# Attention halves in two pieces, value sums queued earlier, and new task rates in a fused attention and two-MLP kernel

## The chip, the core and the metric

The kernel runs as one program on one core of a Trainium2 chip. The metric is the device time of one execution in microseconds. Before the change the median of three runs is 1530.74 us (1528.70, 1530.74 and 1532.65).

## The reference

```
# q, k, v: 8 batches x 8 heads x 576 tokens x 64
k_p, v_p = means of k and v over groups of 8 tokens      # 72 rows each
attn = softmax(q @ k_p^T / 8)                            # 576 x 72 for each head
x = attn @ v_p, heads side by side                       # 4608 tokens x 512
x2 = ((x @ w1) * (x @ w2)) @ w3 @ w_out                  # 512 -> 1024 -> 1024 -> 512
out = square(relu(x2 @ w_in)) @ w_out2                   # 512 -> 2048 -> 512
```

All inputs and the output are float32.

## The kernel before

Tokens are worked on in 9 blocks of 512 (TB). Most products are made of three matmuls of a split operand: a value is a rounded part and a rest, each in the format F32R, and high x high, high x rest and rest x high are added up (mm3). Before anything else, w3 and w_out are folded into one matrix (fold). Then each block goes through the first MLP: stage_ab makes the two products with w1 and w2 (ps_w, 8 units of 48 matmuls), and stage_w multiplies with the folded matrix (acc, 12 matmuls a unit, two units later). After the ninth block comes the second MLP, with the lines L1117 and L1219; no attention work is left then.

Attention fills x between the blocks' matmuls. A batch has 576 tokens and a block has 512, so their borders don't agree. A batch is cut into two halves of 256 and 320 tokens, five query tiles in all. For a query tile there are two score tasks (pe_s: 4 matmuls ps_s each, maxima on DVE at L482, exponentials on ACT at L485) and two transposing tasks (pe_t: ps_t at L521 and L526). For a half there are four AV tasks (pe_av), one for each pair of heads: three matmuls with the split of v (vl, L193) and one with rows of v that don't fit in 128 partitions (vr, L541). Their result is copied by ACT (L554) and subtracted by DVE (L557) into x, which is done apart for each block that the half touches. ps_s, ps_t and ps_av share two PSUM buffers (ps_at).

All order is made while the program is written out. The matmuls of the blocks call tick() after each six. A tick adds `rate` to a credit (attend, L658); from a credit of `visit` on (2.0 while the blocks run), tasks are taken from the front of one list while the credit lasts, one credit each. A task has conditions in a set of things issued, and a task at the front whose condition is not met holds all that stand behind it. An AV task's conditions are ("v", b), that v of its batch has been cut into vl and vr, and ("ab", n), that block n has been issued: x has buffers for two blocks, so the tokens of block m wait for block m - 2. The condition is taken from the half's last token:

```
need = [("v", b)]
last = (b * S + s_end(hf) - 1) // TB
if last >= 2:
    need.append(("ab", last - 2))
```

A block begins when all AV tasks that touch its tokens have been issued (tokens_ready, L674); until then bare ticks are made, which bring tasks alone. The compiler may move instructions of one engine past each other where their data allow it.

v is prepared by kv_parts and load_v (L357): one part at a tick, from a queue that k shares, loads a tile of v (SP's queue) or sums one over groups of 8 (DVE, L329; the odd rows at L325). cut (L366) and cut_odd (L370) then split the sums into vl and vr on ACT (L362, L375) and DVE (L363). load_v(b + 1) is called behind the last AV of batch b (L645). The buffers of raw tiles (three) are shared with the loads of the second MLP's weights, which are converted on ACT and DVE beside the blocks and stored by SP.

The rate is 0.5 at the end of the folding, 0.7 from the point at which block 0 can begin, and 0.6 from the end of block 1 on.

Of the kernel before, what the change touches and what calls it, by code (L numbers as in the profile page):

```python
# [16 lines left out]
TB = 512  # L17
# [18 lines left out]
def attn_moe_moe2_kernel(  # L36
# [17 lines left out]
    B, H, S, D = q.shape  # L54
# [6 lines left out]
    NP = H // 2  # L61
# [8 lines left out]
    QT = []  # L70
    s0 = 0
# [3 lines left out]
    HALF = [[0, 1], [2, 3, 4]]  # L75
    HWS = [sum(QT[i][1] for i in h) for h in HALF]
# [23 lines left out]
    done = set()  # L100
# [85 lines left out]
    def mm3(ps, pairs, first=True, last=True):  # L186

        todo = []
        for (ah, al), (bh, bl) in pairs:
            todo += [(ah, bh), (ah, bl), (al, bh)]  # L190
        n = len(todo)
        return [
            (lambda a=a, b=b, i=i: nc.tensor.matmul(  # L193
                ps, a, b, start=first and i == 0, stop=last and i == n - 1))
            for i, (a, b) in enumerate(todo)
        ]
# [48 lines left out]
    vp = at_p.tile([P, NP, D], F32, tag="vp", name="vp")  # L245
# [4 lines left out]
    vr = at_p.tile([RR, NP, 2, D], F32R, tag="vr", name="vr")  # L250
# [106 lines left out]
    def load_v(b):  # L357


        def parted(hi, lo, src, row):  # L360

            nc.scalar.activation(hi, src, ACTF.Copy, scale=row)  # L362
            nc.vector.scalar_tensor_tensor(  # L363
                lo, src, row, f32(hi), op0=ALU.mult, op1=ALU.subtract)

        def cut():  # L366
            for x in range(2):
                parted(vl[:, 0, :, x, :], vl[:, 1, :, x, :], vp, rows[:, x:x + 1])

        def cut_odd():  # L370
            vo = vr.rearrange("p (a b) t d -> p b a t d", a=2)[:, :, :, 1]
            for x in range(2):
                row = rows[:RB, 2 + x:3 + x]
                parted(vo[:RB, x], vo[2 * RB:, x], v5, row)
                nc.scalar.activation(vo[RB:2 * RB, x], v5, ACTF.Copy, scale=row)  # L375
            done.add(("v", b))

        return kv_parts(v, b, lambda j: vp[:, j, :], [cut, cut_odd])

    def pe_kt(b, part):  # L380

# [148 lines left out]
        if 2 * len(QT) <= g < NG - 1:  # L530
            place_rem(g + 1)

    def pe_av(b, hf, hp):
        hi, lo, rem = atts[b, hf]
        s0 = QT[HALF[hf][0]][0]
        w = sum(QT[i][1] for i in HALF[hf])
        ps = ps_at.tile([P, TB], F32, tag="at", name="ps_av")
        st = [vl[:, i, hp].rearrange("p a d -> p (a d)") for i in range(2)]
        for m in mm3(ps[:, :w], [(st, [t[:, hp, :w] for t in (hi, lo)])], last=False):
            m()  # L540
        nc.tensor.matmul(  # L541
            ps[:, :w], vr[:, hp].rearrange("p a d -> p (a d)"), rem[:, hp // 2, :w],
            start=False, stop=True)
        t0 = b * S + s0
        pieces = []
        o = 0
        while o < w:
            blk, c = divmod(t0 + o, TB)
            n = min(w - o, TB - c)
            pieces.append((blk, c, o, n))  # L550
            o += n

        for blk, c, o, n in pieces:
            nc.scalar.copy(xt_tile(blk, hp)[:, 0, c:c + n], ps[:, o:o + n])  # L554
        for blk, c, o, n in pieces:
            t = xt_tile(blk, hp)
            nc.vector.tensor_sub(t[:, 1, c:c + n], ps[:, o:o + n], f32(t[:, 0, c:c + n]))  # L557
        done.add(("av", b, hf, hp))

    NG = B * len(QT)  # L560

    def s_end(hf):
        return QT[HALF[hf][-1]][0] + QT[HALF[hf][-1]][1]

    def build_tasks(first_k, first_v):


        order = []
        pend = []

        def put(fn, need=()):
            order.append((need, fn))

        def put_pend(n=1):
            for _ in range(min(n, len(pend))):
                order.append(pend.pop(0))

        def kt(b):
            for part in range(2):
                put(lambda part=part: pe_kt(b, part), [("k", b)])  # L580

        def sc(g):
            for half in range(2):
                put(lambda half=half: pe_s(g, half))
                put_pend()

        def turns(g):
            b, i = divmod(g, len(QT))
            for hf, tiles in enumerate(HALF):
                if b < EARLY and i == tiles[0]:  # L590
                    for x in tiles:
                        put(lambda hf=hf, x=x: turn_q(b, hf, x))

        def ahead_of(g):
            b, i = divmod(g, len(QT))
            at = (len(QT) if b + 1 < EARLY else HALF[1][0], len(QT))
            early = b + 1 < EARLY
            if i + 1 == at[0] and b + 1 < B:
                put(lambda b=b: load_q(b + 1, 0))
            if i + 1 == at[1] and b + 1 < B:  # L600
                if not early:
                    put(lambda b=b: load_q(b + 1, 1))
                kt(b + 1)
            if g + 1 < NG:
                turns(g + 1)
                sc(g + 1)
            if i + 1 == at[1] and early:
                put(lambda b=b: load_q(b + 1, 1))

        for fn in first_k:  # L610
            put(fn)
        kt(0)
        turns(0)
        sc(0)
        for g in range(NG):
            b, i = divmod(g, len(QT))
            hf = 0 if i in HALF[0] else 1

            if g < 2 * len(QT):
                if g + 1 != len(QT):  # L620
                    ahead_of(g)
            else:
                if g == 2 * len(QT):
                    ahead_of(g)
                if g + 1 < NG:
                    ahead_of(g + 1)
            if i == HALF[hf][0]:
                put_pend(len(pend))
            for part in range(2):
                put(lambda g=g, part=part: pe_t(g, part))  # L630
                put_pend()
            if g == 0:
                for fn in first_v:
                    put(fn)
            if i == HALF[hf][-1]:
                need = [("v", b)]

                last = (b * S + s_end(hf) - 1) // TB
                if last >= 2:
                    need.append(("ab", last - 2))  # L640
                for hp in range(NP):
                    def av(b=b, hf=hf, hp=hp):
                        pe_av(b, hf, hp)
                        if hf == 1 and hp == NP - 1 and b + 1 < B:
                            load_v(b + 1)  # L645
                    pend.append((need, av))
                if b < EARLY:
                    put_pend(len(pend))
            if g + 1 == len(QT):
                ahead_of(g)  # L650
        put_pend(len(pend))
        return order

    credit = [0.0]
    rate = [0.0]
# [17 lines left out]

    def tokens_ready(n):  # L674

        b, s = divmod(n, S)
        halves = [(bb, h) for bb in range(b) for h in range(2)]
        if s:
            halves.append((b, 0))
            if s > QT[HALF[1][0]][0]:  # L680
                halves.append((b, 1))
        return all(("av", bb, h, hp) in done for bb, h in halves for hp in range(NP))


    wt = {}
# [311 lines left out]
    last = NB - 1  # L997
# [334 lines left out]
    hold_v[0] = False  # L1332
    pumps.append(feed_w12)
    until(lambda: tokens_ready(TB))
    rate[0] = 0.7
    visit[0] = 2.0

    late = []
# [26 lines left out]
    for step in order:  # L1365
# [4 lines left out]
        elif step[0] == "ph":  # L1370
            names, x = plain_units(step[2])
            useq.extend([(n, x) for n in names])
    pend = []
    for i in range(NB):
        until(lambda: tokens_ready((i + 1) * TB))
        keep_q[0] = i > 0
        for u in range(U1):
            stage_ab(i, u)
            if i == last and u == TB // P - 1:
                for n in ("B11", "T1", "T2", "T3"):  # L1380
                    for x in range(2):
                        x2o[n, x] = w0_p.tile([P, 2, TB], F32R, tag="w", name="x2o")
                raw_x.append(x_p.tile([P, 2, TB], F32, tag="x", name="x2r"))
                for n in ("B21", "B22", "T4"):
                    for x in range(2):
                        x2o[n, x] = x_p.tile([P, 2, TB], F32R, tag="x", name="x2o")
                more = x_p.tile([P, 2, TB], F32, tag="x", name="gx")
                operands.extend(operands_of(0))
                tail = operands[-2:]
                del operands[-2:]  # L1390
            if len(pend) == LAG:
                stage_w(*pend.pop(0))
            pend.append((i, u))
        done.add(("ab", i))
        if i == 1:
            rate[0] = 0.6
        if i == 0:
            until(lambda: not fh1)
            sec_p.release()
            ring.append(tc.alloc_tile_pool(name="ring", bufs=RING, reuse_waits="tile"))  # L1400
# [104 lines left out]
```

## Time and profile before

| what | us |
|---|---|
| median of three runs | 1530.74 |
| the profiled execution, time | 1529.85 |
| its span | 1528.0 |
| TensorE (PE) busy | 1492.2 |
| VectorE (DVE) busy | 1000.3 |
| ScalarE (ACT) busy | 798.4 |
| GpSimd (POOL) busy | 81.2 |

Times in the trace count from the span's start. A row of the timeline gives the start, the duration of a group of like instructions, the engine, the line, the operation, what it writes and reads, the shape and the number; in brackets stands how long the engine was idle before it and what it waited for. PEld is TensorE's loading of weights, which lies beside its matmuls. PEclk is the granted share of TensorE's clock.

### The profile page before, as it was taken

The numbers are of one execution on the slowest core, as the hardware profiler recorded it, in microseconds if no ns is written. First come the engines' busy times: TensorE is split into PE (matmuls) and PEld (weight loads), VectorE is DVE, ScalarE is ACT, GpSimd is POOL, SyncE is SP. The second block draws the span as 40 slices with busy tenths as digits, with TensorE's granted clock in tenths as the row PEclk, the third lists the DMA queues.
The fourth block names the chain that finished last, engine by engine and source line by source line (L and its number), as shares of the span: only waits on it lengthen the run. The fifth ranks groups of instructions, "written<-read, shape, count | busy, mean of one in ns | idle before, by whom it ended". The sixth has DMA issues, their size and how long they took to land.

```text
span 1528.0 us, 21290 instructions
## 1 busy us (share of the span) xinstructions
PE 1492.2 (98%) x6752; PEld 1200.6 (79%) x6752; DVE 1000.3 (65%) x1798; ACT 798.4 (52%) x1953; POOL 81.2 (5%) x144
## 2 busy tenths in 40 slices
PE   6899999999999999999999999999999999999998
PEld 3457778877888888878888888888888888888887
DVE  7988686676767477658245477759675967576542
ACT  6866465454545355545235575456445744464431
POOL 1011110101010011100000000000000000000000
PEclk9999999999999999999999999999999999999999
DMA  9545666566666657557539777777777777788752
GB/s 288 197 139 138 165 196 161 168 178 174 187 199 174 193 127 242 149 169 227 173 113 307 222 195 247 208 209 229 235 207 208 232 207 207 208 268 282 209 163 89
DMA packets 292783, 301.34 MB, mean 197 GB/s; under 512 B 119360, under 2 KB 184896, under 8 KB 292672
## 3 DMA queue, kind: packets, MB, share of 16 engines
q1 hardware_dynamic: 287488, 290.54, 65.3%
q10 hardware_dynamic: 5184, 9.44, 1.8%
q8 instruction: 55, 0.90, 0.2%
q14 instruction: 56, 0.46, 0.1%
HBM read 243.27 MB, written 56.62 MB: 196 GB/s over the span
## 4 chain that ended last, share of the span: by engine, by line
PE 71%; DVE 4%; ACT 2%; DMA 1%; issue 1%; ACTq 0%; DVEq 0%
PE o L1219 18%; PE ps_w L193 17%; PE acc L193 9%; PE ps_c L1117 5%; PE ps_a L1117 5%; PE ps_d L1117 5%; PE ps_h L193 3%; PE o L193 3%; PE ps_b L1117 3%; PE ps_s L468 1%; PE ps_av L193 1%; PE ps_t L521 1%; DVE gt L121 1%; DMA rq<-in_moe_w_in_dram 0%; ACT x2o L120 0%
## 5 line engine op out<-in xcount | busy, mean ns | idle before, releaser
L1219 PE MATMUL o<-gt,un 128*128 128x512 f32 x1344 | 329.4, 390 | 0.4
L1219 PEld LDWEIGHTS o<-gt,un 128*128 128x128 f32 x1344 | 251.9, 188 | 54.6 <-DVE gt L121 2.1
L121 DVE TENSOR_TENSOR gt<-gs,gt 128x512 fp32r<-128x512 f32 x240 | 164.9, 689 | 179.8 <-ACT gt L120 178.4
L193 PE MATMUL ps_w<-x,wt 128*128 128x512 f32 x960 | 240.7, 397 | 1.9 <-DVE x L557 0.9
L120 ACT CAST gt<-gs 128x512 fp32r<-128x512 f32 x240 | 148.5, 620 | 154.8 <-PE o L1219 88.0
L193 PE MATMUL acc<-gt,Wt 128*128 128x512 f32 x864 | 219.6, 397 | 0.0
L193 PEld LDWEIGHTS ps_w<-x,wt 128*128 128x128 f32 x960 | 175.5, 188 | 41.2 <-DVE x L557 2.7
L193 PEld LDWEIGHTS acc<-gt,Wt 128*128 128x128 f32 x864 | 160.6, 189 | 32.8 <-issue 0.8
L193 PE MATMUL ps_w<-x,un 128*128 128x512 f32 x768 | 184.5, 392 | 0.0
L193 PEld LDWEIGHTS ps_w<-x,un 128*128 128x128 f32 x768 | 142.5, 188 | 29.1 <-issue 0.2
L485 ACT ACTIVATE att<-ps_s,mx 128x72 f32<-128x72 f32 (+1 forms) x320 | 97.9, 323 | 49.0 <-DVE mx L483 48.6
L1124 ACT ACTIVATE r<-r 128x512 f32<-128x512 f32 x96 | 60.7, 632 | 118.8 <-DVE r L1154 118.3
L844 DVE TENSOR_TENSOR gf<-asb,ps_w 128x512 f32<-128x512 f32 x72 | 49.3, 685 | 75.1 <-PE ps_w L193 68.8
L1117 PE MATMUL ps_a<-x2o,un 128*128 128x512 f32 x384 | 97.5, 389 | 0.0
L1117 PE MATMUL ps_d<-x2o,un 128*128 128x512 f32 x384 | 97.5, 389 | 0.0
L1117 PE MATMUL ps_c<-x2o,un 128*128 128x512 f32 x384 | 97.5, 389 | 0.0
L1125 ACT ACTIVATE gs<-r 128x512 f32<-128x512 f32 x144 | 89.9, 629 | 3.6 <-DMA x2r<-x2d 2.0
L120 ACT CAST gt<-gf 128x512 fp32r<-128x512 f32 x72 | 44.8, 622 | 82.5 <-DVE gf L844 82.2
L1193 DVE TENSOR_TENSOR gs<-gs 128x512 f32<-128x512 f32 x128 | 86.5, 684 | 0.0
L1117 PEld LDWEIGHTS ps_d<-x2o,un 128*128 128x128 f32 x384 | 72.1, 188 | 15.0
L1117 PEld LDWEIGHTS ps_a<-x2o,un 128*128 128x128 f32 x384 | 72.1, 188 | 14.9
L1117 PEld LDWEIGHTS ps_c<-x2o,un 128*128 128x128 f32 x384 | 72.1, 188 | 14.9
(114 smaller groups left out, 1975.2 us busy)
## 6 DMA issues: line engine op xcount, KB each, us to landing
un<-u_w SPq DMA_DIRECT2D x128, 256.0 KB, 3.4
un<-u_A SPq DMA_DIRECT2D x128, 256.0 KB, 3.0
un<-u_S SPq DMA_DIRECT2D x128, 256.0 KB, 3.0
un<-u_oS SPq DMA_DIRECT2D x128, 256.0 KB, 3.0
un<-u_oA SPq DMA_DIRECT2D x96, 256.0 KB, 3.0
raw<-in_moe_w_dram SPq DMA_DIRECT2D x32, 512.0 KB, 5.3
raw<-in_moe_w_out_dram SPq DMA_DIRECT2D x24, 512.0 KB, 4.6
kv<-in_k_dram SPq DMA_DIRECT2D x32, 256.0 KB, 3.3
```

Source lines behind the costliest of these rows:

```text
L120: nc.scalar.copy(hi, src)
L121: return (eng or nc.vector).tensor_sub(lo, src, f32(hi))
L193: (lambda a=a, b=b, i=i: nc.tensor.matmul(ps, a, b, start=first and i == 0, stop=last and i == n - 1))
L468: nc.tensor.matmul(ps[:n, x * 2 * SP:(x + 1) * 2 * SP], t[:, hp, c0:c0 + n], kbd[:, hp].rearrange("p a s -> p (a s)"), start=True, stop=True)
L485: nc.scalar.activation(av[:, h0 + h], sv[:, h], ACTF.Exp, bias=mx[:n, h:h + 1], scale=scale, accum_out=sm[:n, h0 + h:h0 + h + 1])
L521: nc.tensor.transpose(ps[:, c, :n], att[g % 3][:n, c * 2 * SP:c * 2 * SP + P], ident[:n, :n])
L844: front["dve"] = nc.vector.tensor_mul(gf, asb, pss[1])
L1117: nc.tensor.matmul(ps, l, r, start=first and j == 0, stop=j == len(todo) - 1, skip_group_check=True)
L1124: nc.scalar.activation(t, src, ACTF.Relu)
L1125: nc.scalar.activation(take(name), t, ACTF.Square)
L1193: d = nc.vector.tensor_sub(src, a, src)
L1219: nc.tensor.matmul(ob[x][o], l, r, start=u == 0 and m != 5 and j == 0, stop=u == NU - 1 and j == 2, skip_group_check=True)
```

## The change

Three things are changed. A half that lies in two blocks, of which the second is block 2 or later, is multiplied with v in two pieces, cut at the border of the blocks; each piece has its own condition, and its tasks take two pairs of heads each, so that there are four as before. load_v(b + 1) is called when v of batch b has been cut; the sums of v are made then, and the cutting is called behind the last AV of the batch before (read_v), or at the end of the sums if these come later. The rate is 0.8 instead of 0.7, and 0.7 instead of 0.6.

```diff
@@ in load_v
             done.add(("v", b))
-
-        return kv_parts(v, b, lambda j: vp[:, j, :], [cut, cut_odd])
+            if b + 1 < B:
+                load_v(b + 1)
+
+        def summed():
+            done.add(("vs", b))
+            if b in cut_now:
+                cut()
+                cut_odd()
+
+        cuts_v[b] = [cut, cut_odd]
+        return kv_parts(
+            v, b, lambda j: vp[:, j, :], [cut, cut_odd] if b == 0 else [summed])
+
+    cuts_v = {}
+    cut_now = set()
+
+    def read_v(b):
+
+        if b + 1 == B:
+            return
+        cut_now.add(b + 1)
+        if ("vs", b + 1) in done:
+            for fn in cuts_v[b + 1]:
+                fn()
@@ before and in pe_av
+    def av_pieces(b, hf):
+
+        t0 = b * S + QT[HALF[hf][0]][0]
+        w = HWS[hf]
+        cut = TB - t0 % TB
+        if cut >= w or (t0 + cut) // TB < 2:
+            return [(0, w)]
+        return [(0, cut), (cut, w - cut)]
+
-    def pe_av(b, hf, hp):
+    def pe_av(b, hf, hp, q0, w):
...
-        for m in mm3(ps[:, :w], [(st, [t[:, hp, :w] for t in (hi, lo)])], last=False):
+        for m in mm3(ps[:, :w], [(st, [t[:, hp, q0:q0 + w] for t in (hi, lo)])], last=False):
@@ in build_tasks
-                need = [("v", b)]
-
-                last = (b * S + s_end(hf) - 1) // TB
-                if last >= 2:
-                    need.append(("ab", last - 2))
-                for hp in range(NP):
-                    def av(b=b, hf=hf, hp=hp):
-                        pe_av(b, hf, hp)
-                        if hf == 1 and hp == NP - 1 and b + 1 < B:
-                            load_v(b + 1)
-                    pend.append((need, av))
+                pieces = av_pieces(b, hf)
+                for q0, w in pieces:
+                    need = [("v", b)]
+                    last = (b * S + s_end(hf) - HWS[hf] + q0 + w - 1) // TB
+                    if last >= 2:
+                        need.append(("ab", last - 2))
+                    for hp in range(0, NP, len(pieces)):
+                        def av(b=b, hf=hf, hp=hp, q0=q0, w=w, n=len(pieces)):
+                            for x in range(hp, hp + n):
+                                pe_av(b, hf, x, q0, w)
+                            if hf == 1 and hp + n == NP and q0 + w == HWS[hf]:
+                                read_v(b)
+                        pend.append((need, av))
@@ where block 0 can begin, and at the end of block 1
-    rate[0] = 0.7
+    rate[0] = 0.8
...
-            rate[0] = 0.6
+            rate[0] = 0.7
```

tokens_ready asks for the pieces that touch the tokens, instead of the halves.

## Rows read from the trace of the kernel before

**Rows 1.** The page: busy time, share of the span and instructions of each engine.
```profile
PE 1492.2 (98%) x6752; PEld 1200.6 (79%) x6752; DVE 1000.3 (65%) x1798; ACT 798.4 (52%) x1953; POOL 81.2 (5%) x144
```

**Rows 2.** Windows: stretches of the span, busy time of each engine; columns in the first row.
```profile
core 0: us, PE busy (x) PEld busy (x) DVE busy (x) ACT busy (x) POOL busy (x), PEclk, DMA share, GB/s
0.00:114.00 114.00, 93.12 (x342) 51.45 (x343) 95.66 (x191) 83.14 (x227) 13.34 (x27) 0.97 0.66 209
114.00:712.00 598.00, 588.08 (x2841) 479.36 (x2840) 405.22 (x833) 312.98 (x1036) 67.86 (x117) 0.99 0.62 176
712.00:1528.00 816.00, 811.02 (x3572) 669.80 (x3570) 499.47 (x775) 402.28 (x691) 0.00 (x0) 1.00 0.71 211
```

**Rows 3.** Waits of PE, whole span: us in total, times, longest us.
```profile
PE ps_av L541 <- DVE vr L363: 2.2, 1, 2.2
...
PE ps_t L521 <- issue: 2.0, 1, 2.0
...
PE ps_s L468 <- ACT att L485: 1.1, 2, 0.9
...
PE ps_av L193 <- DVE vl L363: 0.9, 2, 0.6
PE ps_w L193 <- DVE x L557: 0.9, 2, 0.5
...
PE ps_av L193 <- DVE x L557: 0.7, 3, 0.3
...
PE ps_av L193 <- ACT vl L362: 0.6, 1, 0.6
```

**Rows 4.** Timeline, 298 to 326 us, all engines.
```profile
317.38 1.89 DVE L325 TENSOR_REDUCE ends<-kv 32x128 f32<-32x1024 f32 x1
...
319.31 0.40 ACT L362 ACTIVATE vr<-ends,rows 32x128 fp32r<-32x128 f32 x1 [2.57 <-DVE ends L325]
...
320.49 0.36 PE L541 MATMUL ps_av<-aR,vr 96*128 96x256 f32 x1 [2.18 <-DVE vr L363]
```

**Rows 5.** Windows of 20 us, columns as in rows 2.
```profile
140.00:160.00 20.00, 17.97 (x86) 14.75 (x85) 19.28 (x39) 10.99 (x35) 2.76 (x4) 0.91 0.64 171
300.00:320.00 20.00, 18.29 (x81) 13.85 (x79) 14.65 (x26) 9.92 (x25) 0.00 (x0) 1.00 0.72 215
320.00:340.00 20.00, 19.51 (x90) 16.24 (x91) 13.49 (x28) 11.38 (x31) 1.99 (x3) 0.91 0.57 151
```

**Rows 6.** Timeline, 133 to 150 us, all engines.
```profile
142.65 0.81 DVE L482 TENSOR_REDUCE mx<-ps_s 128x4 f32<-128x288 f32 x2
...
147.08 1.02 PE L521 MATMUL ps_t<-ident,att 128*128 128x128 f32 x4 [2.03 <-issue]
```

**Rows 7.** Timeline of PE: AV of 256 and 320 columns, two head pairs.
```profile
686.06 0.51 PE L193 MATMUL ps_av<-aT,vl 128*128 128x256 f32 x3
...
686.53 0.52 PE L193 MATMUL ps_av<-aT,vl 128*128 128x256 f32 x3
...
704.39 0.60 PE L193 MATMUL ps_av<-aT,vl 128*128 128x320 f32 x3
...
704.98 0.61 PE L193 MATMUL ps_av<-aT,vl 128*128 128x320 f32 x3
```

**Rows 8.** Groups by form, PEld: busy us, mean ns, idle before and releasers.
```profile
L468 PEld LDWEIGHTS ps_s<-kbd,qT 128*128 128x128 f32 x256 | 38.3, 194 | 6.7 <-issue 1.9 <-ACT qT L421 0.7 <-ACT att L485 0.7
...
L468 PEld LDWEIGHTS ps_s<-kbd,qT 128*64 128x64 f32 x64 | 7.0, 136 | 5.4 <-issue 2.1 <-ACT att L485 1.1 <-DVE aR L529 1.0
```

**Rows 9.** Timeline of PE: plain f32 transposes of 128 columns.
```profile
690.98 0.60 PE L521 MATMUL ps_t<-ident,att 128*128 128x128 f32 x4
691.41 0.38 PE L526 MATMUL ps_t<-ident,rem 128*96 128x128 f32 x2
```

**Rows 10.** Groups by form, DVE, 114 to 712 us: the sums of v.
```profile
L329 DVE TENSOR_REDUCE vp<-kv 128x64 f32<-128x512 f32 x28 | 29.2, 1069 | 1.5 <-DMA kv<-in_v_dram 1.4
...
L325 DVE TENSOR_REDUCE ends<-kv 32x128 f32<-32x1024 f32 x7 | 13.6, 1943 | 0.2 <-DMA kv<-in_v_dram 0.2
```

More of the change, by code (lines that the diff above doesn't have):

```diff
@@ L531, in pe_t @@
             place_rem(g + 1)
-    def pe_av(b, hf, hp):
+    def av_pieces(b, hf):
[6 more added lines that the diff above has]
+    def pe_av(b, hf, hp, q0, w):
         hi, lo, rem = atts[b, hf]
-        s0 = QT[HALF[hf][0]][0]
-        w = sum(QT[i][1] for i in HALF[hf])
+        s0 = QT[HALF[hf][0]][0] + q0
         ps = ps_at.tile([P, TB], F32, tag="at", name="ps_av")
         st = [vl[:, i, hp].rearrange("p a d -> p (a d)") for i in range(2)]
-        for m in mm3(ps[:, :w], [(st, [t[:, hp, :w] for t in (hi, lo)])], last=False):
+        for m in mm3(ps[:, :w], [(st, [t[:, hp, q0:q0 + w] for t in (hi, lo)])], last=False):
             m()
         nc.tensor.matmul(
-            ps[:, :w], vr[:, hp].rearrange("p a d -> p (a d)"), rem[:, hp // 2, :w],
+            ps[:, :w], vr[:, hp].rearrange("p a d -> p (a d)"), rem[:, hp // 2, q0:q0 + w],
             start=False, stop=True)
@@ L557, in pe_av @@
             nc.vector.tensor_sub(t[:, 1, c:c + n], ps[:, o:o + n], f32(t[:, 0, c:c + n]))
-        done.add(("av", b, hf, hp))
+        done.add(("av", b, hf, hp, q0))
     NG = B * len(QT)
@@ L674, in tokens_ready @@
     def tokens_ready(n):
[L676 to L682, printed above, removed]
+        for b in range(B):
+            for hf in range(2):
+                t0 = b * S + QT[HALF[hf][0]][0]
+                for q0, w in av_pieces(b, hf):
+                    if t0 + q0 < n and any(
+                            ("av", b, hf, hp, q0) not in done for hp in range(NP)):
+                        return False
+        return True
     wt = {}
```

## The prediction

> **What bounds the kernel now.** I read the engine totals first: TensorE is busy for 98% of the span, the next engine for 65% [rows 1]. So only two things can move the time: work added to TensorE, and idle time or slow clock taken from it. The stretches say where that idle time lies [rows 2]. From 712 us on TensorE is busy for 811.0 of 816 us and no attention work is left. Before 114 us (weight folding, block 0's attention) it loses 20.9 us, but there the change alters no piece (the half that straddles blocks 0 and 1 stays whole, since the second piece's block is below 2) and the new rates are not set yet. The stretch that the change can reach is 114 to 712 us, and there TensorE idles 598 - 588.1 = 9.9 us. That, with two dips of the clock, is all that can be won.
>
> The list of waits then names the idle time [rows 3]. Waits for v: 2.2 us on vr (L363), 0.9 us in two on vl (L363), 0.6 us on vl (L362), together 3.7 us. The largest is seen whole in the timeline [rows 4]: the sum of v's odd rows (1.89 us on DVE) ends at 319.3, ACT and DVE cut it, and the fourth matmul of an AV group, at the head of TensorE's queue, starts at 320.49 after 2.18 us of nothing. Right behind it the granted clock is 0.91 over 20 us, where it was 1.00 [rows 5]; with levels of 2.4 and 1.2 GHz that is 0.09 x 2 x 20 = 3.6 us at half clock, so 1.8 us lost. Waits where a block begins, since its tokens come from a half that was let go only when the block before had been issued: 0.9 us on x (L557) by ps_w, 0.7 us on x by ps_av, and 0.9 of the 1.1 us on att (L485), together 2.5 us. A third kind is the 2.0 us of ps_t at 145 to 147 us: the maxima that ACT's exponentials need were late on DVE, the two ps_at buffers stayed held, and 0.91 of clock followed [rows 5, 6]. It cost 2.0 + 1.8 = 3.8 us.
>
> **The pieces: added work on TensorE.** A half's first token is 576b or 576b + 256, and its width is 256 or 320. By that, six halves straddle with a second block of 2 or more, and are cut into these widths: batch 1 192 + 128, batch 2 128 + 192, batch 3 64 + 256 (each from 320), batch 5 192 + 64, batch 6 128 + 128, batch 7 64 + 192 (each from 256). Each has four head pairs, and each piece of each pair takes four matmuls with their own weight loads: 6 x 4 x 4 = 96 matmuls more. The columns streamed stay the same, and so do ACT's and DVE's evacuations, since those were split by block already.
>
> What a matmul of under 256 columns costs in this precision no row shows. The rows nearby: four matmuls of 256 columns take 686.53 - 686.06 = 0.47 us, four of 320 take 704.98 - 704.39 = 0.59 us, that is 117.5 and 147.5 ns each [rows 7]. A line through both passes within 3 ns of zero, so if columns alone count, splitting adds nothing: lower end 0 us. But each piece loads 128 weight columns again. Loads of 128 columns for ps_s last 194 ns and loads of 64 last 136 ns [rows 8], so 64 columns occupy 58 ns and 128 occupy an estimated 116 ns. If loads follow each other no closer than that, a piece of 64 or 128 or 192 columns takes 116 ns. Then the halves of 256 cost 8 x 116 - 470 = 458 ns more for each pair, 192 + 128 from 320 costs 928 - 590 = 338, and 64 + 256 costs 464 + 470 - 590 = 344. The sum is 4 x (3 x 458 + 2 x 338 + 344) = 9.6 us. Upper end: if a narrow piece runs at the pace of the plain f32 transposes, (691.41 - 690.98) / 4 = 108 ns for 128 columns or 0.84 ns a column [rows 9], a piece of 192 takes 162 ns and the sum is 4 x (2 x 642 + 458 + 2 x 522 + 344) = 12.5 us. I take 9.6 us, since the load rows are of the operation that repeats.
>
> The Trainium skill, "TensorE: Matmul & The Clock Gate", section "LDWEIGHTS (loading the stationary operand)", speaks against the pieces in the same way: a load takes its columns divided by 1.2 ns, whatever the contraction, an estimate of 107 ns here, by which the added work would be 8.0 us. The trace's pair of rows gives 116, and I keep that.
>
> The order of tasks grows by nothing: four AV tasks a half before, two pieces of two tasks after. A task now brings two head pairs, whose PSUM tiles fill both ps_at buffers; that is no denser than the present pairs of tasks at 686 and 704 us, which run without a gap [rows 7]. Cost 0; its upper end is inside the rival on stalls.
>
> What the pieces remove: the first piece lies in an earlier block, so it waits only for the block two before that one, which is long issued, and the next block can be begun as soon as the last has been issued. The waits at block starts, 2.5 us, go. If the rate does not bring the first piece in time, they stay: 0 to 2.5 us; I take 2.5, since rate and condition both move that way.
>
> **v sooner.** load_v(b + 1) now enters the queue of loads when v of b has been cut, instead of after the last AV of b. So its five loads and sums run one half to one batch ahead; what is left for the moment of need is the cutting, called right behind the last AV of the batch. All issues move with it: six DMAs on SP's queue (five tiles, the odd one in two), which pass stores and weight loads of the second stage; per batch four sums of 1.07 us and one of 1.94 us on DVE [rows 10], 6.2 us. The number is the same, and keys are ahead of v in the queue as before. DMA engines are busy for 62% of 114 to 712 us and DVE for 405 of 598 us [rows 2], so room hides them; if not, the price is the third kind of stall. The cutting comes in one tick where it took two; the next batch's AVs are several tasks away, so 0. The waits for v go: 3.7 us, and the dip behind the largest, 1.8 us. Together 5.5 us, and at least the 2.2 + 1.8 = 4.0 us of the largest. Next late in its place are the exponentials of the same tile, which tasks behind AV wait for anyway.
>
> **Rates 0.8 and 0.7.** Tasks are taken in pairs when credit reaches 2, so a pair comes each 2.5 ticks instead of 2.86, and 2.86 instead of 3.33. The number of tasks is the same, and AV stops at a block's condition in both kernels. More density can't win more than the idle time counted, and can add stalls of the third kind. The one at 145 us can vanish (-3.8) or be doubled (+3.8); I take 0.
>
> **The sum**, against the profiled execution (span 1528.0, time 1529.85; the median of the runs is 0.9 us above it): +9.6 - 5.5 - 2.5 = +1.6 us, so 1531.45; I forecast 1531.5. A difference under 0.3%, 4.6 us, can't be told from none.
>
> **Rivals.**
> First, faster: narrow pieces cost by columns alone, the loads hide behind the matmuls before, and all counted waits go: 0 - 8.0, so 1521.9. For it: loads of 188 to 194 ns already overlap matmuls that are 117 ns apart [rows 7, 8]. Against it: those loads then overlap only each other. Chance 0.24. The Trainium skill, same page, section "Back-to-back issue gap", supports this one: the gap is the columns divided by 2.4 plus 2.5 ns, which would make 96 more matmuls an estimated 0.24 us; but the trace's 117.5 ns at 256 columns is 8 ns above that formula's 109.
> Second, slower: the denser tasks and v's sums meet DVE where it is fullest, 19.28 of 20 us at 140 to 160 us [rows 5]; maxima come late, both ps_at buffers stay held, and the stall of 145 us is repeated. It decides from two such stalls on, 7.6 us: 1.6 + 7.6 = +9.2, so 1539.0. For it: one stands there already, at a rate of 0.7, and 6.2 us of sums for batch 2 move from behind 200 us into block 0. Against it: after 190 us DVE has room and PE waits for no maxima. Chance 0.20.
> Third, the change doesn't do what it says at the block starts: the first piece still comes only when the block before has been issued, since tasks ahead of it are late; 9.6 - 5.5 = +4.1, so 1534.0. Or the narrow pieces run at plain f32's pace: 12.5 - 8.0 = +4.5, so 1534.3. Against the former: AV tasks now stand at the block's condition with all tasks before them done. Together 0.13.
>
> **How the numbers follow.** The forecast has 0.43. Slower by over 0.3% (above 1535.3): the second rival and 0.05 of the third, 0.25. Faster (below 1526.1): the first and 0.05 of the forecast's lower side, 0.29. Within: 0.46. The range goes from 1522 to 1538: it leaves out about half of the first rival and half of the second. The forecast's own range is 1527 to 1535.
>
> **What would show it.** In the trace of after, ps_av has 96 more matmuls in forms of 64, 128 and 192 columns; their spacing decides between 116 ns (forecast), columns alone (first rival) and 162 ns at 192 columns. TensorE's waits for vr and vl should be gone after 200 us, and the clock 1.00 at 320 us; the waits for x where blocks 3 and 6 begin should be gone. New waits of ps_t or ps_s for ACT's exponentials, with clock under 1.00, would show the second rival. The forecast is wrong if the pieces are cheaper than 5 us or if more than one such stall appears.

## The result, and the profile after

The change makes the kernel slower: 1549.55 us (median of 4 runs, 1546.90 to 1550.96) against 1530.83 us, ratio 1.0121 with a 95% interval of 1.0102 to 1.0140. That is 18.7 us more, outside the range of 1522 to 1538 us, and on the side that had a chance of 0.25.

The page after, first part, and the windows over the stretches that answer to [rows 1] and [rows 2]; attention ends at 730 us instead of 712 us.

```profile
PE 1501.8 (97%) x6848; PEld 1208.6 (78%) x6848; DVE 1001.9 (65%) x1798; ACT 797.8 (51%) x1953; POOL 86.0 (6%) x144
```

```profile
0.00:112.00 112.00, 89.80 (x338) 49.42 (x339) 95.68 (x190) 82.25 (x225) 13.34 (x27) 0.98 0.68 213
112.00:730.00 618.00, 598.31 (x2935) 488.67 (x2935) 401.53 (x822) 310.63 (x1034) 72.66 (x117) 0.99 0.59 169
730.00:1549.20 819.20, 813.73 (x3579) 670.49 (x3577) 504.67 (x787) 404.93 (x697) 0.00 (x0) 1.00 0.71 211
```

TensorE has exactly 96 matmuls more, and DVE and ACT the same number of instructions. In the stretch with attention TensorE is busy for 10.2 us more (598.31 against 588.08 in [rows 2]), and idle for 618 - 598.31 = 19.7 us, where it was 9.9. So the idle time that was to shrink has doubled. The waits of PE, over the whole span, say with what (columns as in [rows 3]):

```profile
PE ps_av L193 <- DVE x L587: 6.6, 8, 2.2
...
PE ps_t L543 <- issue: 4.0, 2, 3.6
...
PE ps_s L490 <- DVE x L587: 1.6, 3, 1.0
PE ps_t L543 <- DVE x L587: 1.3, 3, 0.7
```

The waits of [rows 3] for vr and vl and those of ps_w for x are gone, as forecast. In their place stand 6.6 + 1.6 + 1.3 = 9.5 us in which ps_av, ps_s or ps_t wait for the copying out of an earlier AV group (x, now L584 on ACT and L587 on DVE): the two ps_at buffers are taken. The timeline of all engines at the longest shows how that goes:

```profile
613.20 0.44 PE L193 MATMUL ps_av<-aT,vl 128*128 128x128 f32 x3
...
613.59 0.50 PE L193 MATMUL ps_av<-aT,vl 128*128 128x128 f32 x3
...
614.66 0.62 ACT L960 CAST oq<-wq 128x512 fp32r<-128x512 f32 x1 [3.09 <-DMA u_S<-oq]
615.18 0.42 ACT L584 CAST x<-ps_av 128x128 fp32r<-128x128 f32 x2
...
616.35 0.28 DVE L587 TENSOR_TENSOR x<-ps_av,x 128x128 fp32r<-128x128 f32 x1
...
616.69 0.55 PE L193 MATMUL ps_av<-aT,vl 128*128 128x128 f32 x3 [2.21 <-DVE x L587]
```

Two narrow groups are through in 0.8 us and hold both buffers; ACT stands for 3.09 us at a conversion of the second MLP's weights that waits for a store, and the two copies come behind it, from 615.18 us on. Whether groups of 256 or 320 columns would have waited here too, no run shows for this place.

The second longest of these waits, 1.82 us, came about in another way:

```profile
479.98 0.70 PE L490 MATMUL ps_s<-kbd,qT 128*64 128x144 f32 x4
480.60 1.97 DVE L325 TENSOR_REDUCE ends<-kv 32x128 f32<-32x1024 f32 x1
480.61 0.58 PE L193 MATMUL ps_av<-aT,vl 128*128 128x192 f32 x3
...
484.13 0.34 DVE L587 TENSOR_TENSOR x<-ps_av,x 128x192 fp32r<-128x192 f32 x1
...
484.52 0.58 PE L193 MATMUL ps_av<-aT,vl 128*128 128x192 f32 x3 [1.82 <-DVE x L587]
```

Here one score tile and one AV group hold the buffers, and DVE has the sum of v's odd rows and four other instructions ahead of the subtraction that TensorE waits for.

The clock goes with these waits: the dip at 320 us that [rows 5] showed is gone, and two others have come, behind the waits at 484 and 616 us.

```profile
320.00:340.00 20.00, 20.00 (x99) 16.47 (x98) 14.08 (x30) 8.11 (x28) 2.54 (x5) 1.00 0.54 135
480.00:500.00 20.00, 18.18 (x78) 14.62 (x78) 18.05 (x35) 9.96 (x24) 1.49 (x1) 0.91 0.78 231
600.00:620.00 20.00, 16.57 (x83) 13.58 (x84) 12.51 (x30) 8.71 (x25) 1.14 (x1) 0.97 0.83 251
620.00:640.00 20.00, 20.00 (x94) 16.29 (x93) 15.54 (x33) 14.96 (x40) 2.11 (x5) 0.94 0.84 280
```

The price of the narrow matmuls themselves is in the timeline of PE, here pieces of 192 and of 64 columns, two head pairs each (the third of 192 columns waits for a buffer):

```profile
284.53 0.47 PE L193 MATMUL ps_av<-aT,vl 128*128 128x192 f32 x3
284.85 0.27 PE L571 MATMUL ps_av<-aR,vr 96*128 96x192 f32 x1
284.95 0.50 PE L193 MATMUL ps_av<-aT,vl 128*128 128x192 f32 x3
...
286.31 0.58 PE L193 MATMUL ps_av<-aT,vl 128*128 128x192 f32 x3 [0.74 <-DVE x L587]
...
528.65 0.49 PE L193 MATMUL ps_av<-aT,vl 128*128 128x64 f32 x3
528.98 0.28 PE L571 MATMUL ps_av<-aR,vr 96*128 96x64 f32 x1
529.09 0.50 PE L193 MATMUL ps_av<-aT,vl 128*128 128x64 f32 x3
```

Four of 192 columns take 0.42 us and four of 64 take 0.44 us, so the columns hardly count. From the start of one AV matmul to that of the next, over all pieces, the median is 112 ns at 64 and 128 columns and 113 ns at 192. With 112 ns in the sum of the prediction the 96 matmuls come to 4 x (3 x 426 + 2 x 306 + 328) = 8.9 us.

### The profile page after: what moved, and what is told of

Same layout as the page of the kernel before. It is cut to its first block, busy times and chain, and to the rows that moved or that the text cites. A ratio compares the mean times of both kernels' runs of the same rounds, so it can differ in the third digit from the quotient of the medians.

```text
span 1549.2 us, 21425 instructions
## 1 busy us (share of the span) xinstructions
PE 1501.8 (97%) x6848; PEld 1208.6 (78%) x6848; DVE 1001.9 (65%) x1798; ACT 797.8 (51%) x1953; POOL 86.0 (6%) x144
## 4 chain that ended last, share of the span: by engine, by line
PE 75%; DVE 10%; DMA 7%; ACT 4%; issue 2%; SPq 1%; DVEq 0%; ACTq 0%
PE ps_w L193 20%; PE o L1252 18%; PE acc L193 9%; PE ps_a L1150 5%; PE ps_c L1150 5%; PE ps_d L1150 5%; PE ps_h L193 3%; PE o L193 3%; PE ps_b L1150 2%; PE ps_s L490 2%; DMA raw<-in_moe_w_out_dram 2%; PE ps_av L193 1%; DMA raw<-in_moe_w_dram 1%; DVE raw L161 1%; ACT att L507 1%
## 5 line engine op out<-in xcount | busy, mean ns | idle before, releaser
L193 PE MATMUL ps_w<-x,wt 128*128 128x512 f32 x960 | 246.5, 402 | 0.6 <-ACT wt L1339 0.4
L193 PE MATMUL acc<-gt,Wt 128*128 128x512 f32 x864 | 216.3, 394 | 0.0
L873 ACT COPY asb<-ps_w 128x512 f32<-128x512 f32 x72 | 42.4, 589 | 96.5 <-PE ps_w L193 96.3
```

Of the source, the lines that this page charges most:

```text
L193: (lambda a=a, b=b, i=i: nc.tensor.matmul(ps, a, b, start=first and i == 0, stop=last and i == n - 1))
L873: nc.scalar.copy(asb, ps)
```

## The experiments

Three theories were tried first. A: two narrow head pairs in one task run out of PSUM buffers. B: the denser tasks bring the loss. C: v's sums, moved, hold up evacuations. Later came D: the order of tasks that the new conditions make brings the waits, whatever the buffers; E: the compiler places the narrow matmuls in another order, and the waits come from that; and F, its rival: the split costs what it costs by its matmuls on the chip. Each ratio is to the kernel before, which ran on the same chip (medians 1529.8 to 1531.2 us).

**One part at a time.** v_only takes halves whole and the old rates:

```diff
-        if cut >= w or (t0 + cut) // TB < 2:
-            return [(0, w)]
-        return [(0, cut), (cut, w - cut)]
+        return [(0, w)]
...
-    rate[0] = 0.8
+    rate[0] = 0.7
...
-            rate[0] = 0.7
+            rate[0] = 0.6
```

> The kernel before with v's sums queued sooner alone (halves whole, rates 0.7 and 0.6). Theory A (the loss comes from the pieces: two narrow head pairs in one task want four PSUM tiles where there are two, so TensorE waits for their evacuation): the waits for v go and nothing else changes, 4 to 6 us faster than before, ratio 0.996 to 0.997. Theory B (the loss comes from the denser tasks): the same, 4 to 6 us faster. Theory C (v's sums, moved, now stand on DVE ahead of evacuations that TensorE waits for): 3 to 8 us slower than before.

Measured: 1527.61 us, ratio 0.9978 (0.9965 to 0.9991). C falls for v sooner by itself, which gains about 3.6 us, a little under the 4 to 6 that A and B foresaw.

pieces_only has the pieces with the old rates and v loaded behind the last AV:

```diff
-            if b + 1 < B:
-                load_v(b + 1)
...
-            v, b, lambda j: vp[:, j, :], [cut, cut_odd] if b == 0 else [summed])
+            v, b, lambda j: vp[:, j, :], [cut, cut_odd])
...
-                                read_v(b)
+                                if b + 1 < B:
+                                    load_v(b + 1)
```

> The kernel before with the pieces alone (v loaded behind the last AV of the batch, rates 0.7 and 0.6). A: about 9 us of narrow matmuls and 6 to 10 us of waits for the two buffers, so 14 to 20 us slower than before, ratio about 1.011. B: the matmuls alone less the waits at block starts, 5 to 8 us slower. C: as B.

Measured: 1565.99 us, ratio 1.0214 (1.0189 to 1.0240), 34.8 us more than before: twice what A foresaw. The waits of its PE show a reason why the loss is greater than in the full change: the pieces also ask for v before it is there, 6.9 us in vl and vr.

```profile
PE ps_av L193 <- DVE x L585: 6.2, 10, 1.6
PE ps_av L193 <- ACT vl L362: 5.0, 2, 3.4
...
PE ps_av L193 <- ACT att L505: 3.2, 2, 1.8
...
PE ps_av L569 <- ACT vr L375: 1.9, 3, 0.7
```

The clock is lower too: its mean was 0.987 to 0.993 in the four runs, and 0.993 to 0.995 in those of the full change.

rates_only is the kernel before with 0.8 and 0.7:

```diff
-    rate[0] = 0.7
+    rate[0] = 0.8
...
-            rate[0] = 0.6
+            rate[0] = 0.7
```

> The kernel before with the rates 0.8 and 0.7 alone. A: within 2 us of before. B: 6 to 12 us slower than before, with waits of ps_s for late queries and of ps_t for late exponentials. C: within 2 us.

Measured: 1530.31 us, ratio 0.9990 (0.9978 to 1.0001). B falls.

after_old_rates is the changed kernel with the two rate lines put back.

> The changed kernel with the old rates 0.7 and 0.6 (pieces and v sooner). A: 10 to 15 us slower than before, within 4 us of the changed kernel. B: at 1534 to 1540 us, 8 us or more faster than the changed kernel. C: within 4 us of the changed kernel, as A; v alone tells these two apart.

Measured: 1555.85 us, ratio 1.0157 (1.0142 to 1.0172), 6 us slower than the full change. The rates help when there are pieces, which none of the three foresaw. Against pieces_only, which differs in v alone, it is 10.1 us faster: v sooner gains beside the pieces as well, so on balance C falls there too, although the wait at 484 us shows its mechanism once.

v_and_rates is the changed kernel without the pieces (the first edit of v_only alone).

> The changed kernel without the pieces: halves whole, v sooner, rates 0.8 and 0.7. If the pieces are the whole loss, 1525 to 1529 us, at or below v sooner alone. If the rates and v sooner together lose something, 1533 us or more.

Measured: 1526.38 us, ratio 0.9967 (0.9956 to 0.9978). The parts add up, 3.6 and 0.9 us, and the pieces are the whole loss: 1549.55 - 1526.38 = 23.2 us, of which the 96 matmuls explain 8.9. v_only and this version are the two that beat both kernels; their intervals overlap.

The profiled executions show where the rest lies. They are further apart than the medians, 1549.2 - 1521.7 = 27.5 us of span. The page of v_and_rates has

```profile
PE 1486.8 (98%) x6752; PEld 1196.5 (79%) x6752; DVE 998.7 (66%) x1798; ACT 797.0 (52%) x1953; POOL 81.0 (5%) x144
```

so TensorE idles 34.9 us there and 47.4 us in the changed kernel: 12.5 us. Its mean clock is 0.999 there and 0.995 in the changed kernel; as shares of the spans that is 1.5 and 7.7 us lost, 6.2 us more (an estimate, which takes TensorE as busy throughout). With 8.9 us of matmuls the three come to 27.6 us.

**What in the pieces costs 23 us.** split_mm leaves tasks, conditions, v, rates and PSUM tiles as before, and only cuts the matmuls of the six halves by columns, within one tile:

```diff
-        for m in mm3(ps[:, :w], [(st, [t[:, hp, :w] for t in (hi, lo)])], last=False):
-            m()
...
+        cut = TB - t0 % TB
+        whole = cut >= w or (t0 + cut) // TB < 2
+        for c0, c1 in [(0, w)] if whole else [(0, cut), (cut, w)]:
+            for m in mm3(ps[:, c0:c1], [(st, [t[:, hp, c0:c1] for t in (hi, lo)])], last=False):
+                m()
...
```

> The kernel before, where only the matmuls of the six straddling halves are cut by columns at the block's border, in the same PSUM tile, the same task and under the same condition: the 96 narrow matmuls by themselves. The trace of the changed kernel has them at a median of 112 to 113 ns each. If that is their price, 8 to 10 us slower than before, ratio about 1.006. Rival: the spacing hides work that is paid anyway and columns alone count, within 2 us of before.

Measured: 1553.82 us, ratio 1.0154 (1.0137 to 1.0171): 23.1 us slower than before, where both guesses were at most 10. Nothing but the width and number of matmuls differs in the source, and their spacing in the trace is again 111 to 114 ns at the median. So 14 us came from elsewhere. The timelines of PE at the start of block 1 show it. The kernel before (320 columns whole):

```profile
194.26 0.72 PE L193 MATMUL ps_av<-aT,vl 128*128 128x320 f32 x3
194.82 1.32 PE L193 MATMUL acc<-gt,Wt 128*128 128x512 f32 x5
196.27 0.42 PE L541 MATMUL ps_av<-aR,vr 96*128 96x320 f32 x1
196.52 0.60 PE L193 MATMUL ps_av<-aT,vl 128*128 128x320 f32 x3
196.96 0.31 PE L541 MATMUL ps_av<-aR,vr 96*128 96x320 f32 x1
197.11 0.71 PE L193 MATMUL ps_w<-x,wt 128*128 128x512 f32 x2
```

split_mm at the same place, timeline of all engines:

```profile
192.00 0.58 PE L193 MATMUL ps_av<-aT,vl 128*128 128x192 f32 x3
...
192.42 0.27 PE L545 MATMUL ps_av<-aR,vr 96*128 96x192 f32 x1
...
192.53 0.47 PE L193 MATMUL ps_av<-aT,vl 128*128 128x128 f32 x3
...
193.98 0.33 PE L545 MATMUL ps_av<-aR,vr 96*128 96x128 f32 x1 [0.98 <-DVE aR L529]
...
195.47 0.58 PE L193 MATMUL ps_av<-aT,vl 128*128 128x192 f32 x3 [0.27 <-DVE x L560]
...
198.08 0.95 PE L193 MATMUL ps_av<-aT,vl 128*128 128x192 f32 x3 [1.50 <-DVE x L560]
```

In the kernel before, blocks' matmuls (acc, ps_w) stand between the AV groups, and the evacuations run under them. In split_mm all eight groups of the half stand on end, with nothing to do while a buffer is copied out. The source gives both the same order of tasks, so the order is the compiler's. Counted in the traces, groups of four AV matmuls stand on end two at most before; in split_mm, where two groups make one head pair, there are one run of eight, two of six and three of four. The changed kernel has three runs of four.

That made theory E: width decides the order. split_as_256 tells it from the chip's price of a split. It has the same split, but each part is 256 columns wide, so columns in both parts are worked out twice (the edit against split_mm):

```diff
-        for c0, c1 in [(0, w)] if whole else [(0, cut), (cut, w)]:
+        for c0, c1 in [(0, w)] if whole else [(0, 256), (w - 256, w)]:
```

> As split_mm, but each of the two parts takes 256 columns: the parts overlap, and the columns in both are worked out twice. At 118 ns a matmul that is 4 x (3 x 472 + 3 x 356) = 9.9 us of matmuls more than before, 1 us more than the narrow ones take in the traces. Theory E (the compiler puts the instructions into another order when these matmuls are narrow, with up to eight AV groups on end where the kernel before has two, and the waits come from that): the order made here has at most four on end, so about the matmuls' own price, 1538 to 1543 us. Theory F (any split of these halves costs what split_mm shows, by its matmuls on the chip): 1552 to 1556 us.

Measured: 1539.77 us, ratio 1.0061 (1.0040 to 1.0082): 14.0 us less than split_mm, with as many matmuls, each streaming more columns. Its timeline at the same place has the blocks' matmuls between the groups again:

```profile
194.00 0.52 PE L193 MATMUL ps_av<-aT,vl 128*128 128x256 f32 x3
194.36 0.28 PE L545 MATMUL ps_av<-aR,vr 96*128 96x256 f32 x1
194.48 0.53 PE L193 MATMUL ps_av<-aT,vl 128*128 128x256 f32 x3
194.84 0.28 PE L545 MATMUL ps_av<-aR,vr 96*128 96x256 f32 x1
194.96 0.86 PE L193 MATMUL ps_w<-x,wt 128*128 128x512 f32 x3
195.66 0.51 PE L193 MATMUL ps_av<-aT,vl 128*128 128x256 f32 x3
```

What it has above the kernel before, 9.3 us, is about the matmuls' own price, 9.9 us at 118 ns. Its waits of ps_av for x are 0.8 us from 120 to 800 us, where split_mm has 4.3. Waits are not all of the difference, as the windows of the stretch with attention show, split_mm first:

```profile
111.00:727.00 616.00, 595.52 (x2897) 486.31 (x2896) 408.86 (x830) 312.13 (x1035) 68.11 (x117) 0.98 0.61 170
111.00:715.00 604.00, 591.79 (x2918) 483.46 (x2917) 404.62 (x831) 313.26 (x1039) 67.61 (x117) 1.00 0.62 175
```

TensorE idles 20.5 us in the one and 12.2 us in the other, and the clock was 0.98 against 1.00. In all four runs of each the mean clock was 0.989 to 0.993 for split_mm and 0.998 to 1.000 for split_as_256; 0.008 of 1540 us is an estimated 12 us. Idle time and clock together come to more than the 14.0 us, so this is rough; but the clock is no smaller a part of it than the waits.

One thing is not held apart here: the second part writes columns again that the first has written, which ties the two together. The next run has no such tie.

after_as_256 does the same in the changed kernel: a piece's matmuls take 256 columns of the half, and only the piece is copied out.

```diff
+        a = min(q0, HWS[hf] - 256) if w < 256 else q0
+        z = max(w, 256)
-        for m in mm3(ps[:, :w], [(st, [t[:, hp, q0:q0 + w] for t in (hi, lo)])], last=False):
+        for m in mm3(ps[:, :z], [(st, [t[:, hp, a:a + z] for t in (hi, lo)])], last=False):
...
+        ps = ps[:, q0 - a:]
```

> The changed kernel, where each narrow piece's matmuls take 256 columns of the half, and only the piece is copied out. E: about 10 us above the kernel without pieces (1526.4), 1535 to 1541 us. F: as the changed kernel, 1547 to 1552 us.

Measured: 1539.65 us, ratio 1.0058 (1.0040 to 1.0077), 9.9 us faster than the changed kernel though it streams more columns. Its groups stand on end two at most, where the changed kernel has runs of four, and its waits of ps_av for x are 3.2 us from 120 to 800 us instead of 6.4. E holds in both kernels.

**The buffers.** after_one_tile puts the two head pairs of a task beside each other in one PSUM tile:

```diff
-        ps = ps_at.tile([P, TB], F32, tag="at", name="ps_av")
+        ps = ps_at.tile([P, TB], F32, tag="at", name="ps_av")
+        for k, hp in enumerate(hps):
+            pk = ps[:, k * w:(k + 1) * w]
...
-                            for x in range(hp, hp + n):
-                                pe_av(b, hf, x, q0, w)
+                            pe_av(b, hf, list(range(hp, hp + n)), q0, w)
```

> The changed kernel, where the two head pairs of a task lie beside each other in one PSUM tile (each piece has at most 256 columns), so a task takes one buffer as before. Theory A (two buffers run out): TensorE's waits of ps_av for x go and the time falls to 1537 to 1543 us, about the matmuls' own 9 us above the kernel with v sooner alone. Theory D (the order that the new conditions make, whatever the buffers): 1546 to 1552 us, as the changed kernel.

Measured: 1542.03 us, ratio 1.0081 (1.0061 to 1.0101), 7.5 us off the changed kernel. That is where A put it. Only 0.2 us is left of the waits of ps_av for x, but 6.4 us of ps_t for x have come instead, waits for a tile that is still being copied out (PE's waits, 120 to 800 us):

```profile
PE ps_t L543 <- DVE x L590: 6.4, 4, 3.2
```

after_single_pair gives each task one head pair, eight tasks for a half that is cut:

```diff
-                    for hp in range(0, NP, len(pieces)):
-                        def av(b=b, hf=hf, hp=hp, q0=q0, w=w, n=len(pieces)):
+                    for hp in range(NP):
+                        def av(b=b, hf=hf, hp=hp, q0=q0, w=w, n=1):
```

> The changed kernel with one head pair in each task of a piece, so eight tasks for a half that is cut instead of four. Theory A: half of the buffer waits go, 1540 to 1546 us. Theory D: as the changed kernel or slower, since more tasks stand in the list, 1547 to 1555 us.

Measured: 1540.16 us, ratio 1.0069 (1.0054 to 1.0084), 9.4 us off the changed kernel. A holds, in so far as the grouping of two pairs is a cost of its own; D falls. But the order has changed here too: groups stand on end two at most, as in after_as_256, though the matmuls are narrow. So narrow matmuls alone don't make the order; the tasks that they come in count as well, and this run doesn't tell the buffers from the order.

one_tile_256 joins after_one_tile and after_as_256.

> The changed kernel with both: two head pairs of a task in one PSUM tile, and each piece's matmuls at 256 columns. Both alone took 7.5 and 9.9 us off the changed kernel. If they take away the same waits for the two buffers, the two together give no more than the better of them: 1537 to 1542 us, the 10 us of the matmuls and some 2 us of waits above the kernel without pieces. If they are two losses, 1530 to 1534 us.

Measured: 1534.93 us, ratio 1.0032 (1.0019 to 1.0044), between the two expectations: 14.6 us off the changed kernel (13.6 when each is taken against the kernel before on its own chip), where the two alone give 7.5 and 9.9. So they take away partly the same waits, and neither alone takes all. What stays above v_and_rates is 8.5 us (about 9.5 by each chip's kernel before), about the price of the matmuls; of the waits for x 1.5 us are left. Both this run and after_one_tile have six runs of four groups on end, so here their number is not what 256 columns change. What is can be seen at one of the six, after_one_tile first:

```profile
609.32 0.80 PE L543 MATMUL ps_t<-ident,att 128*128 128x128 f32 x4 [3.16 <-DVE x L590]
```

```profile
604.33 1.09 PE L193 MATMUL ps_w<-x,wt 128*128 128x512 f32 x4
605.67 0.63 PE L543 MATMUL ps_t<-ident,att 128*128 128x128 f32 x4 [0.24 <-DVE x L592]
```

With 256 columns four of the block's matmuls stand between the four groups and the transposes that need a buffer; with narrow matmuls the transposes come right behind the groups, and wait 3.16 us.

## Why the prediction was wrong

The step that failed is in the part on the pieces: "A task now brings two head pairs, whose PSUM tiles fill both ps_at buffers; that is no denser than the present pairs of tasks at 686 and 704 us, which run without a gap [rows 7]. Cost 0". It costs about 14 us: 23.2 us of the pieces less 8.9 of matmuls, and 14.6 us come back when width and buffers are both changed (one_tile_256). Three things were overlooked. The groups at 686 and 704 us stand in pairs with matmuls of the blocks behind each pair, and I took that filling as given; it is made by the compiler, and with narrow matmuls it is made otherwise. Two narrow groups are through in 0.8 us, and the next one wants a buffer before ACT and DVE have copied the first out (0.74 us of waiting at 286 us, 2.21 at 616 us). And the sum has no clock for waits that the pieces would add, though it prices the clock behind the old ones: in the profiled executions the clock is 6.2 us of the loss, beside 12.5 us of idle time.

Point by point. The matmuls: right, 9.6 us forecast and 8.9 worked out from the spacing after; the row of the shorter weight loads gave 116 ns and the trace 112, although the row is of loads for ps_s. The Trainium skill's rule that I set beside it ("TensorE: Matmul & The Clock Gate", "LDWEIGHTS (loading the stationary operand)") gives 107 ns, and the trace agrees within about 5 ns: pieces of 64, 128 and 192 columns cost the same, as they should if the loads set the pace.

v sooner: mechanism right, gain too large. All waits for v of [rows 3] went, and the dip of the clock with them; measured alone 3.6 us instead of 5.5, and under the 4.0 that I had as the least.

The block starts: the waits of ps_w for x went (forecast 2.5 us), but the pieces gave the time back at the buffers. With pieces the next block does begin sooner: from the start of block 4's last ps_w matmul to that of block 5's first it is 3.0 us (523.2 to 526.2 us) instead of 4.2 us (515.5 to 519.7). A block has 192 ps_w matmuls in the traces (8 units of 24, not of 48). At every border but the first it is 3.0 us in the changed kernel, where the kernel before has 3.0 to 8.1. So the third rival's first half is wrong.

The rates: alone 0.9 us faster and not distinguishable from none, forecast 0. With pieces they gain 6 us, which was not foreseen; why they do was not tried apart.

The first rival, that loads hide, is wrong: columns don't count below 256. Its support, the Trainium skill's "TensorE: Matmul & The Clock Gate", section "Back-to-back issue gap", gives 56 ns for 128 columns, but for a matmul by itself; for a stream of loads and matmuls the same section has about 81 ns, which the prediction left out. The trace has 112, and the measurement decides. The second rival had the right sign but the wrong place: its stall at 145 us is there in after (3.6 of the 4.0 us of ps_t), but much the same stands in v_and_rates, which is faster than before. The buffers that it named as held by the exponentials are mostly held by the pieces' evacuations.

What stays open is why the compiler orders narrow matmuls differently. after_as_256 against the changed kernel, and split_as_256 against split_mm, show that the width changes the order; after_single_pair shows that the grouping of the tasks does too. The compiler's reason was not tried. Nor was the loss parted between order, buffers and what else ACT and DVE have in hand at the time. The second MLP took 707.9 us instead of 706.3, from the last ps_w of block 8 to the last matmul, and loads of its weights came later than before (the last of w_in was issued at 548 us instead of 489); that was not tried apart either.

## What to carry to other kernels

Where a compiler orders the instructions, the price of an operation is not only its own time: before splitting one, look in the built order at what now stands between its parts, and whether the buffers and evacuations behind it had been covered by other work. Price a new wait with the clock that may fall behind it. Count buffers against groups in flight, not against tasks. And take a bundle apart: two of the three parts here gain 4.4 us together, and the third loses 23.

## What was not expected of the hardware

In this precision a matmul that loads 128 weight columns took 112 ns at 64, 128 and 192 columns alike, and 118 ns at 256: below 256 columns nothing was saved. To split a half's matmuls into two of 256 columns was cheaper for the kernel than to split them into narrower ones, by 14.0 us over six halves (split_as_256 against split_mm), though by the order and the clock that came with them. The clock fell behind waits of TensorE of 1.82 and 2.21 us in the changed kernel (0.91 over 480 to 500 us, 0.94 over 620 to 640 us), but stayed at 1.00 behind one of 3.03 us in v_only (140 to 160 us).
